# One-tile chunks, two hidden blocks in a PSUM bank and epsilon as a column of the masked sum, in top-k attention followed by an MLP

## The chip, the cores and the metric

The kernel runs on one core of one Trainium2 chip. The metric is the device time in microseconds; the time before is the median of three runs. The profile is one execution of the program taken by the hardware profiler. TensorE (PE) multiplies matrices, its weight loads are listed apart (PEld); VectorE (DVE), ScalarE (ACT) and GpSimd (POOL) work elementwise, and SyncE (SP) issues the transfers.

## The reference

Top-32 attention over 8 batches of 8 heads, 576 queries and keys, head dimension 64; the result, as 4608 tokens of 512, goes through an MLP of 2048 hidden units with a piecewise activation. Everything is float32.

```python
# q, k, v: (8, 8, 576, 64); w_in: (512, 2048); w_out: (2048, 512)
scores = scale * np.matmul(q, k.transpose(0, 1, 3, 2))
kth = np.partition(scores, -32, axis=-1)[..., -32:-31]
scores = np.where(scores >= kth, scores, -1e9)
attn = np.exp(scores - np.max(scores, axis=-1, keepdims=True))
attn = attn / (np.sum(attn, axis=-1, keepdims=True) + 1e-09)
x = np.matmul(attn, v)                    # then (B,H,S,D) -> (B*S, H*D)
h = x @ w_in
g = np.where(h >= 1, h, np.where(h <= -1, 0.0, (h + 1) ** 2 / 4))
out = g @ w_out
```

## The kernel before

A **step** treats one tile of 128 queries and two heads (a tail tile gathers the last 64 queries of two batches). There are 144 steps. In a step TensorE makes the scores, ScalarE scales them and takes the exponentials, VectorE finds the 32nd largest of each row, masks and sums, GpSimd divides by the sum, a transfer through DRAM transposes the weights, and TensorE multiplies by the values. Four steps (two for a tail tile) fill one tile `xT` of 128 tokens, and the MLP of that tile is then queued as small pieces of work, which are issued between the steps that follow. The weights of the MLP and some inputs arrive as 64-bit words and are converted during the first steps. The order on each engine is fixed when the program is built.

The top-k on VectorE works on half-width tiles: `more` is the larger, later the smaller, of two halves of the scores.

```python
nc.vector.tensor_tensor(out=more, in0=s[:, :, 0:SH], in1=s[:, :, SH:S], op=ALU.max)     # L294
nc.vector.max(out=eight(tops, i, 0), in_=more[:, i, :])                                  # L305, x2
for r in range(8, TOP_K, 8):                                                             # three rounds
    nc.vector.match_replace(...)                                                         # L321, x2
    nc.vector.max(out=eight(tops, i, r), in_=src[:, i, :])                               # L330, x2
nc.vector.tensor_tensor(out=less, in0=s[:, :, 0:SH], in1=s[:, :, SH:S], op=ALU.min)      # L332
nc.vector.max(...)                                                                       # L335, x2
nc.vector.tensor_tensor_scan(out=kth, ...)                                               # L337
for i in range(2):                                                                       # masked sum
    nc.vector.scalar_tensor_tensor(out=e[:, i, :], in0=s[:, i, :], scalar=last[i], in1=e[:, i, :],
                                   op0=ALU.is_ge, op1=ALU.mult, accum_out=z[:, i:i + 1]) # L344
nc.vector.tensor_scalar(z, z, 1e-9, None, ALU.add)                                       # L349
nc.vector.reciprocal(rz, z)                                                              # L350
# ... GpSimd: e *= rz (L357); ScalarE: two copies of e as 16-bit halves (L386); transfers (L388, L389)
```

The scores go through PSUM tiles of two banks, twice a step; the values and the MLP's first products share a pair of banks.

```python
sp = ps.tile([P, 2, BANK], F32, name="sp", tag="a", bufs=2)     # scores; transposes use the same tag
po = ps.tile([P, P], F32, name="po", tag="ph", bufs=2)          # values (L403, L411)
```

The MLP of a chunk, which is one tile or two:

```python
def hidden(f, c0, c1):                                          # block f of 128 hidden units
    ph = ps.tile([P, CW], F32, name="ph", tag="ph", bufs=2)[:, 0:c1 - c0]
    for kk in range(NK):                                        # L433
        nc.tensor.matmul(ph, w_in[:, kk, f * P:(f + 1) * P], xT[:, kk, c0:c1], ...)
    nc.scalar.activation(r, ph, AF.Relu, bias=half, scale=0.5)  # L437
    nc.scalar.activation(g, ph, AF.Relu, bias=minus, scale=1.0) # L445
    nc.gpsimd.tensor_scalar(r, r, 1.0, 0.0, ALU.min, ALU.max)   # L450
    nc.gpsimd.tensor_tensor(out=r, in0=r, in1=r, op=ALU.mult)   # L451
    nc.gpsimd.tensor_tensor(out=g, in0=r, in1=g, op=ALU.add)    # L452

def final(f):
    for i in range(len(tiles)):                                 # L458; py: a pair of banks
        nc.tensor.matmul(pys[i], gs[f][:, i * P:(i + 1) * P], w_out[:, f, :], ...)
        # after the last f: y = copy of py by ScalarE (L462), then the store

for x in range(NF + LAG):      # LAG = 4: final(x - 4) goes with hidden(x)
    ...
```

A matmul of float32 shows as two records in the trace, each with its weight load. In the values below, a unit is one product of 128 x 128 x 128: `hidden` of one tile has 4, `final` of one tile has 4, a tile has 128 and the program 4608.

Of the kernel before, what the change touches and what calls it, by code (L numbers as in the profile page):

```python
# [24 lines left out]
def kernel(  # L25
# [27 lines left out]
    NF = DFF // P  # L53
    CT = 2
    CW = CT * P
    LAG = 4
# [21 lines left out]
    for i in range(2):  # L78
        v_tails.append([const.tile([P, H, D], F32, name=f"v_tail{i}{x}") for x in range(2)])
        for x in v_tails[i]:  # L80
            nc.gpsimd.memset(x, 0.0)


# [83 lines left out]
    def run(ctx, paired):  # L167
        xtp = ctx.enter_context(tc.tile_pool(name="xtp", bufs=3))
        stage = ctx.enter_context(tc.tile_pool(name="stage", bufs=2))
# [97 lines left out]
        def scores(st):  # L267
            t, hp, kT, qT = st["t"], st["hp"], st["keys"]["kT"], st["qT"]
            st["s"] = s = att.tile([P, 2, S], F32, name="s", bufs=3)
            for hf in range(2):  # L270
                sp = ps.tile([P, 2, BANK], F32, name="sp", tag="a", bufs=2)
                c0, c1 = hf * SH, (hf + 1) * SH
                for i in range(2):
                    for j in ([i] if t < NT else [0, 1]):
                        d = slice(j * D, (j + 1) * D)
                        g = hp if t < NT else hp + i
                        o = sp[:, i] if t < NT else sp[j * TL:(j + 1) * TL, i]
                        for a0, a1, k0 in pieces(i, j, c0, c1):
                            nc.tensor.matmul(o[:, a0 - c0:a1 - c0], qT[d, g, :], kT[d, g, k0:k0 + a1 - a0],  # L279
                                             start=True, stop=True)  # L280
                nc.scalar.activation(s[:, :, c0:c1], sp[:, :, 0:SH], AF.Copy, scale=SCALE)  # L281
# [15 lines left out]
        def first_top(st):  # L297
            s = st["s"]
            if paired:
                pairs(st)  # L300
            st["tops"] = tops = att.tile([P, 2 * TOP_K], F32, name="tops", bufs=3)
            st["e"] = e = att.tile([P, 2, S], F32, name="e", bufs=3)
            nmax = att.tile([P, 2], F32, name="nmax")
            for i in range(2):
                nc.vector.max(out=eight(tops, i, 0), in_=(st["more"] if paired else s)[:, i, :])  # L305
            nc.scalar.activation(nmax, tops[:, 0:2 * SPLIT:SPLIT], AF.Copy, scale=-1.0)
            for i in range(2):
                nc.scalar.activation(e[:, i, :], s[:, i, :], AF.Exp, bias=nmax[:, i:i + 1])  # L308
                yield


        def weights(st, after):
            s, m, tops, e = st["s"], st["m"], st["tops"], st["e"]
            kth = att.tile([P, LAST + 1], F32, name="kth", bufs=3)
# [28 lines left out]
            for i in range(2):  # L343
                nc.vector.scalar_tensor_tensor(out=e[:, i, :], in0=s[:, i, :], scalar=last[i],  # L344
                                               in1=e[:, i, :], op0=ALU.is_ge, op1=ALU.mult,
                                               accum_out=z[:, i:i + 1])
            yield
            rz = att.tile([P, 2], F32, name="rz")
            nc.vector.tensor_scalar(z, z, 1e-9, None, ALU.add)  # L349
            nc.vector.reciprocal(rz, z)  # L350
            if st["by_tensor"]:
                st["rz"] = diag = (late or words).tile([P, 2, P], F32, name="diag", bufs=1)
                for i in range(2):
                    nc.scalar.activation(diag[:, i, :], ident, AF.Copy, scale=rz[:, i:i + 1])
            else:
                for i in range(2):
                    nc.gpsimd.tensor_scalar(e[:, i, :], e[:, i, :], rz[:, i:i + 1], 1.0, ALU.mult, ALU.mult)  # L357
            if paired:
# [36 lines left out]
        def values(st):  # L395
            t, hp, v_in, v_tl = st["t"], st["hp"], st["keys"]["v"], st["keys"]["v_tl"]
            wT = st["wT"]
            po = ps.tile([P, P], F32, name="po", tag="ph", bufs=2)
            if t < NT:
# [26 lines left out]

        def mlp(xT, tiles, pool, last):
            gs, pys = {}, {}

            def hidden(f, c0, c1):  # L430
                ph = ps.tile([P, CW], F32, name="ph", tag="ph", bufs=2)[:, 0:c1 - c0]
                for kk in range(NK):
                    nc.tensor.matmul(ph, w_in[:, kk, f * P:(f + 1) * P], xT[:, kk, c0:c1],  # L433
                                     start=(kk == 0), stop=(kk == NK - 1))

                r = pool.tile([P, CW], F32, name="r", bufs=2)[:, 0:c1 - c0]
                nc.scalar.activation(r, ph, AF.Relu, bias=half, scale=0.5)  # L437
                gs[f] = pool.tile([P, CW], F32, name="g", bufs=2 * LAG)
                g = gs[f][:, c0:c1]
                if last:  # L440
# [4 lines left out]
                nc.scalar.activation(g, ph, AF.Relu, bias=minus, scale=1.0)  # L445
                if converted < n_pieces and f % 2:
                    nc.scalar.activation(r, r, AF.Square)
                    nc.gpsimd.tensor_scalar(r, r, 1.0, 0.0, ALU.min, ALU.max)
                else:
                    nc.gpsimd.tensor_scalar(r, r, 1.0, 0.0, ALU.min, ALU.max)  # L450
                    nc.gpsimd.tensor_tensor(out=r, in0=r, in1=r, op=ALU.mult)  # L451
                nc.gpsimd.tensor_tensor(out=g, in0=r, in1=g, op=ALU.add)  # L452

            def final(f):
                for i in range(len(tiles)):
                    if f == 0:
                        pys[i] = ps.tile([P, DM], F32, name="py", tag="py", bufs=2)
                    nc.tensor.matmul(pys[i], gs[f][:, i * P:(i + 1) * P], w_out[:, f, :],  # L458
                                     start=(f == 0), stop=(f == NF - 1))
                    if f == NF - 1:  # L460
                        y = (late or words).tile([P, DM], F32, name="y", bufs=2)
                        nc.scalar.copy(y, pys[i])  # L462
                        for p0, p1, rows in rows_of(*tiles[i]):
                            nc.sync.dma_start(out=rows, in_=y[p0:p1])


            n_tiles, work = len(tiles), []
            for x in range(NF + LAG):
                if x < NF:
                    work.append((NK * n_tiles, needed(x, False), partial(hidden, x, 0, n_tiles * P)))  # L470
                if x >= LAG:
                    work.append((n_tiles * DM // P, needed(x - LAG, True), partial(final, x - LAG)))
            return work


        rounds, chunks = [], []
        for b in range(0, B, 2):
            a, c, tl = [(b, t) for t in range(NT)], [(b + 1, t) for t in range(NT)], (b, NT)
            rounds += a + [tl, (b + 1, NT)] + c
            if 0 < b and b + 2 < B:  # L480
                chunks += [a[0:2], a[2:4], [tl]] + ([c[0:2], c[2:4]] if b + 4 < B else [[x] for x in c])
            else:
                chunks += [[x] for x in a + [tl] + c]
        steps = []
        for b, t in rounds:
            tile_of = (b, t) if t < NT else (b - b % 2, t)
            ch = next(n for n, tiles in enumerate(chunks) if tile_of in tiles)
            col = chunks[ch].index(tile_of) * P + (TL if t == NT and b % 2 else 0)
            for hp in (range(NHP) if t < NT else range(0, NHP, 2)):
                steps.append((b, t, hp, ch, col))  # L490
# [7 lines left out]
        pending = deque()  # L498
        total, spent = sum(len(tiles) for tiles in chunks) * (NK * NF + NF * DM // P), 0
        converted, inspected, due = 0, 0, 0.0  # L500
# [28 lines left out]
        def advance(amount, until):  # L529
# [4 lines left out]
            while pending:  # L534
                cost, pieces, work = pending[0]
                if pieces > converted or usable[pieces] > pe_time + 0.5:
# [44 lines left out]
        def begin(m):  # L581
            b, t, hp, ch, col = steps[m]
            if ch not in xTs:
                xTs[ch] = xtp.tile([P, NK, CW], F32, name="xT")
            state.append(dict(m=m, t=t, hp=hp, keys=keys[b], qT=qTs[b, t], xT=(xTs[ch], col)))
# [27 lines left out]
        def values_until(m):  # L613
            nonlocal valued, pe_time
            while valued < min(m, n):
# [3 lines left out]
                if valued in ready:  # L619
                    ch = ready[valued]  # L620
                    pending.extend(mlp(xTs[ch], chunks[ch], mlp_pool, ch == len(chunks) - 1))
                valued += 1

        first_late = None
        for m in range(n + 2):
# [8 lines left out]
            for r in sorted(ready):  # L634
                if r + 3 > m and r >= valued:
                    share = min(share, left / (r + 3 - m))
                    left += len(chunks[ready[r]]) * (NK * NF + NF * DM // P)
            top_k, parts = None, [0] * SLOTS
# [8 lines left out]
            for slot in range(SLOTS):  # L647
# [24 lines left out]
                if slot == 4:  # L672
                    begin_at(m + 2)
                if slot == 5 and not early:
                    values_until(m - 1)
                if slot == (6 if early else 1):
# [63 lines left out]
```

## Time and profile before

| | before |
|---|---|
| median of three runs | 1665.99 us (1664.15 to 1668.44) |
| span of the profiled execution | 1666.6 us |
| mean granted TensorE clock | 0.972 |
| PE / PEld busy | 1540.7 / 1057.8 us |
| DVE busy | 1532.8 us |
| ACT busy | 1208.2 us |
| POOL busy | 1041.8 us |
| mean transfer rate | 137 GB/s |

A group line of the profile has the kernel's line, engine and operation, output and inputs, shape and count; after the bar the busy time and the mean length of one in ns; after the second bar the engine's idle time ahead of it and what ended it. Where instructions of an engine overlap, the busy time counts the overlap once. A line of the list of waits has the waiting engine and line, what ended the wait, the total in us, the number of waits and the longest. Line numbers are those of the kernel before unless another is named.

### The profile page before, as it was taken

Reading aid. Unit: us, or ns where it says so; the run is one execution under the profiler, and the core shown is the slowest. Engines: PE = TensorE matmul, PEld = TensorE weight load, DVE = VectorE, ACT = ScalarE, POOL = GpSimd, SP = SyncE. Lnnn points to the kernel's source line nnn. Section 1 sums busy time; section 2 is a strip of 40 time slices with the busy share of each in tenths; the row PEclk is TensorE's granted clock in tenths of the full one; section 3 lists DMA queues with packets and bytes.
Section 4 is the critical chain, followed back from the end, with each engine's and each line's share of the span. In section 5 each row is a group of like instructions: output and inputs, shape, how many; then the busy total and the mean of one; then the engine's idle time right before and its main releaser. Section 6 shows DMA issues by size and latency. Waiting matters only on the chain.

```text
span 1666.6 us, 32108 instructions
## 1 busy us (share of the span) xinstructions
PE 1540.7 (92%) x10157; PEld 1057.8 (63%) x10157; DVE 1532.8 (92%) x4587; ACT 1208.2 (72%) x2680; POOL 1041.8 (63%) x1918
## 2 busy tenths in 40 slices
PE   6586999999999999999999999999999999999998
PEld 4464666666666666666566666666666666666665
DVE  6999999999999999999999999999989998999942
ACT  5686677777777876787677777777777776777743
POOL 4675676666667645565454545577766676777750
PEclk6798999999999999999999999999999999999999
DMA  8333256555455556555555556545554544445420
GB/s 249 114 99 98 80 143 171 146 151 148 141 150 144 158 138 173 161 149 143 134 160 163 141 140 178 155 135 135 127 156 124 146 124 124 132 124 129 109 64 16
DMA packets 439061, 227.91 MB, mean 137 GB/s; under 512 B 393056, under 2 KB 401248, under 8 KB 438880
## 3 DMA queue, kind: packets, MB, share of 16 engines
q1 hardware_dynamic: 438880, 225.75, 49.7%
q8 instruction: 82, 1.34, 0.3%
q14 instruction: 99, 0.81, 0.2%
HBM read 62.91 MB, written 86.11 MB: 89 GB/s over the span
## 4 chain that ended last, share of the span: by engine, by line
PE 38%; DVE 37%; ACT 14%; POOL 5%; issue 4%; DMA 1%; SPq 0%; POOLq 0%; DVEq 0%; ACTq 0%
PE ph L433 15%; PE py L458 14%; DVE more L321 9%; DVE tops L330 8%; DVE e L344 6%; ACT halves L386 4%; PE sp L279 4%; PE po L403 4%; DVE seconds L335 3%; DVE more L332 3%; DVE tops L305 3%; ACT e L308 3%; DVE more L294 3%; POOL e L357 2%; ACT s L281 2%
## 5 line engine op out<-in xcount | busy, mean ns | idle before, releaser
L433 PEld LDWEIGHTS ph<-xT,w_in 128*128 128x128 f32 x3840 | 531.0, 193 | 222.7 <-issue 99.6
L433 PE MATMUL ph<-xT,w_in 128*128 128x128 f32 (+1 forms) x3840 | 604.6, 304 | 47.2 <-ACT g L445 43.4
L458 PE MATMUL py<-w_out,g 128*128 128x512 f32 x1152 | 573.4, 604 | 1.7 <-POOL w_out L146 0.9
L450 POOL TENSOR_SCALAR r<-r 128x128 f32<-128x128 f32 (+1 forms) x456 | 187.0, 410 | 408.7 <-ACT r L437 407.6
L437 ACT ACTIVATE r<-ph,half 128x128 f32<-128x128 f32 (+1 forms) x480 | 186.9, 389 | 273.9 <-PE ph L433 228.0
L321 DVE MATCH_REPLACE8 more<-tops,more 128x288 f32<-128x288 f32 x864 | 375.7, 442 | 0.0
L330 DVE MAX8 tops<-more 128x8 f32<-128x288 f32 x864 | 349.1, 445 | 0.0
L452 POOL TENSOR_TENSOR g<-r,g 128x128 f32<-128x128 f32 (+1 forms) x464 | 277.6, 598 | 36.4
L386 ACT COPY halves<-e 128x1152 uint16<-128x1152 uint16 x260 | 287.1, 1155 | 15.5 <-POOL e L357 14.7
L458 PEld LDWEIGHTS py<-w_out,g 128*128 128x128 f32 x1152 | 192.4, 191 | 117.6 <-issue 87.9
L451 POOL TENSOR_TENSOR r<-r 128x128 f32<-128x128 f32 (+1 forms) x456 | 239.2, 525 | 38.0
L344 DVE SCALAR_TENSOR_TENSOR e<-s,kth,e 128x576 f32<-128x576 f32 x288 | 249.9, 904 | 6.0
L357 POOL TENSOR_SCALAR e<-e,rz 128x576 f32<-128x576 f32 x260 | 215.1, 838 | 49.5 <-DVE rz L350 49.5
L308 ACT ACTIVATE e<-s,nmax 128x576 f32<-128x576 f32 x288 | 218.5, 770 | 4.7
L445 ACT ACTIVATE g<-ph,minus 128x128 f32<-128x128 f32 (+1 forms) x464 | 179.6, 387 | 0.0
L281 ACT ACTIVATE s<-sp 128x576 f32<-128x576 f32 x288 | 169.6, 640 | 5.4 <-PE sp L279 5.4
L279 PE MATMUL sp<-kT,qT 64*128 64x288 f32 x1024 | 163.1, 436 | 9.4 <-ACT kT L239 8.5
L403 PE MATMUL po<-wT,v_in 128*64 128x128 f32 x2048 | 143.9, 280 | 16.5 <-ACT g L445 11.3
L403 PEld LDWEIGHTS po<-wT,v_in 128*64 128x64 f32 x2048 | 111.4, 137 | 70.6 <-issue 21.7
L279 PEld LDWEIGHTS sp<-kT,qT 64*128 64x128 f32 x1024 | 90.2, 189 | 84.3 <-issue 52.3
L294 DVE TENSOR_TENSOR more<-s 128x576 f32<-128x576 f32 x144 | 112.4, 780 | 23.9 <-ACT s L281 23.5
L335 DVE MAX8 seconds<-more 128x8 f32<-128x288 f32 x288 | 118.3, 452 | 14.0
(89 smaller groups left out, 1331.0 us busy)
## 6 DMA issues: line engine op xcount, KB each, us to landing
rows<-halves SPq DMA_DIRECT2D x130, 576.0 KB, 2.8
raw<-in_moe_w_out_dram SPq DMA_DIRECT2D x52, 256.0 KB, 3.0
raw<-in_moe_w_in_dram SPq DMA_DIRECT2D x48, 256.0 KB, 3.0
k_in<-in_k_dram SPq DMA_DIRECT2D x64, 128.0 KB, 3.1
q_in<-in_q_dram SPq DMA_DIRECT2D x32, 256.0 KB, 3.3
v_in<-in_v_dram SPq DMA_DIRECT2D x8, 1024.0 KB, 6.4
out_dram<-y SPq DMA_DIRECT2D x32, 256.0 KB, 3.0
kT<-in_moe_w_in_dram SPq DMA_DIRECT2D x16, 256.0 KB, 4.2
```

The source lines that it names most:

```text
L279: nc.tensor.matmul(o[:, a0 - c0:a1 - c0], qT[d, g, :], kT[d, g, k0:k0 + a1 - a0], start=True, stop=True)
L308: nc.scalar.activation(e[:, i, :], s[:, i, :], AF.Exp, bias=nmax[:, i:i + 1])
L321: nc.vector.match_replace(out=rest[:, i, :], in_to_replace=eight(tops, i, r - 8), in_values=src[:, i, :], imm_value=LOWEST)
L330: nc.vector.max(out=eight(tops, i, r), in_=src[:, i, :])
L344: nc.vector.scalar_tensor_tensor(out=e[:, i, :], in0=s[:, i, :], scalar=last[i], in1=e[:, i, :], op0=ALU.is_ge, op1=ALU.mult, accum_out=z[ ...
L357: nc.gpsimd.tensor_scalar(e[:, i, :], e[:, i, :], rz[:, i:i + 1], 1.0, ALU.mult, ALU.mult)
L386: nc.scalar.copy(halves[:, :, i * S:(i + 1) * S], st["e"][:, i, :].bitcast(U16).rearrange("p (k t) -> p t k", t=2))
L403: nc.tensor.matmul(po[j * D:(j + 1) * D], v_in[:, h, c, :] if c < NT else v_tl[0][:, h, :], wT[:, block(j, c)], start=(c == 0), stop=(c == ...
L433: nc.tensor.matmul(ph, w_in[:, kk, f * P:(f + 1) * P], xT[:, kk, c0:c1], start=(kk == 0), stop=(kk == NK - 1))
L451: nc.gpsimd.tensor_tensor(out=r, in0=r, in1=r, op=ALU.mult)
L452: nc.gpsimd.tensor_tensor(out=g, in0=r, in1=g, op=ALU.add)
L458: nc.tensor.matmul(pys[i], gs[f][:, i * P:(i + 1) * P], w_out[:, f, :], start=(f == 0), stop=(f == NF - 1))
```

## The change

It has five parts.

1. **Chunks of one tile.** Before, the tiles of the middle batches went two at a time through the MLP, so that ScalarE and GpSimd worked on 256 columns, and the others alone with 128. Now all go alone.
2. **Two blocks in a bank.** `hidden` makes two blocks of 128 hidden units side by side in one PSUM bank, and ScalarE and GpSimd treat both in one instruction of 256 columns. The last tile keeps single blocks. The lag of four now counts groups of two.
3. **One unbroken stream, three banks.** The last second products of a tile are laid between the first groups of the next. Values and first products share three banks instead of two; second products have one instead of two.
4. **Values next to scores.** In the later part a step's values are issued directly behind scores, a slot earlier than before.
5. **Epsilon as a column.** The score and weight tiles get a column 576, with the largest number and 1e-9, set once; the masked sum runs over 577 columns, and the separate addition goes.

The diff, cut to its core:

```diff
-    CT = 2
-    CW = CT * P
+    GROUP = 2
...
+    scores_of, weights_of = [[const.tile([P, 2, S + 8], F32, name=f"{x}{i}") for i in range(3)] for x in ("s", "e")]
+    for i in range(3):
+        nc.gpsimd.memset(scores_of[i][:, :, S:S + 1], LARGEST)
+        nc.gpsimd.memset(weights_of[i][:, :, S:S + 1], 1e-9)
...
-                nc.vector.scalar_tensor_tensor(out=e[:, i, :], in0=s[:, i, :], scalar=last[i],
-                                               in1=e[:, i, :], op0=ALU.is_ge, op1=ALU.mult,
+                nc.vector.scalar_tensor_tensor(out=st["all"][1][:, i, :], in0=st["all"][0][:, i, :], scalar=last[i],
+                                               in1=st["all"][1][:, i, :], op0=ALU.is_ge, op1=ALU.mult,
                                                accum_out=z[:, i:i + 1])
             yield
             rz = att.tile([P, 2], F32, name="rz")
-            nc.vector.tensor_scalar(z, z, 1e-9, None, ALU.add)
             nc.vector.reciprocal(rz, z)
...
-            po = ps.tile([P, P], F32, name="po", tag="ph", bufs=2)
+            po = ps.tile([P, P], F32, name="po", tag="ph", bufs=3)
...
-            def hidden(f, c0, c1):
-                ph = ps.tile([P, CW], F32, name="ph", tag="ph", bufs=2)[:, 0:c1 - c0]
-                for kk in range(NK):
-                    nc.tensor.matmul(ph, w_in[:, kk, f * P:(f + 1) * P], xT[:, kk, c0:c1],
-                                     start=(kk == 0), stop=(kk == NK - 1))
+            def hidden(x):
+                ph = ps.tile([P, group, P], F32, name="ph", tag="ph", bufs=3)
+                for i in range(group):
+                    f = x * group + i
+                    for kk in range(NK):
+                        nc.tensor.matmul(ph[:, i], w_in[:, kk, f * P:(f + 1) * P], xT[:, kk],
+                                         start=(kk == 0), stop=(kk == NK - 1))
...
-                        pys[i] = ps.tile([P, DM], F32, name="py", tag="py", bufs=2)
+                    py.append(ps.tile([P, DM], F32, name="py", tag="py", bufs=1))
...
+            behind = []
+            while pending and pending[-1][3]:
+                behind.insert(0, pending.pop())
+            for x in range(NF // group + LAG):
+                if x < NF // group:
+                    pending.append((NK * group, needed(x * group + group - 1, False), partial(hidden, x), False))
+                if x < LAG:
+                    for _ in range(min(GROUP, len(behind))):
+                        pending.append(behind.pop(0)[0:3] + (False,))
+                else:
+                    for f in range((x - LAG) * group, (x - LAG + 1) * group):
+                        pending.append((DM // P, needed(f, True), partial(final, f), x >= NF // group))
...
-            if 0 < b and b + 2 < B:
-                chunks += [a[0:2], a[2:4], [tl]] + ([c[0:2], c[2:4]] if b + 4 < B else [[x] for x in c])
-            else:
-                chunks += [[x] for x in a + [tl] + c]
+            chunks += a + [tl] + c
...
                 if slot == 4:
                     begin_at(m + 2)
-                if slot == 5 and not early:
-                    values_until(m - 1)
+                    if not early:
+                        values_until(m - 1)
```

## The prediction

> **What bounds the kernel now.** I read the busy table first, then the busy time by stage, then the waits of the late stage, then VectorE's instructions one by one.
>
> ```profile
> PE 1540.7 (92%) x10157; PEld 1057.8 (63%) x10157; DVE 1532.8 (92%) x4587; ACT 1208.2 (72%) x2680; POOL 1041.8 (63%) x1918
> ```
>
> TensorE and VectorE stand at the same 92%, so the page alone does not say which one sets the pace. The view by stage does better (its columns: stretch, then busy us of PE, PEld, DVE, ACT, POOL, then clock and DMA):
>
> ```profile
> 0.00:200.00 200.00, 142.27 (x919) 106.95 (x920) 183.00 (x528) 135.74 (x332) 123.39 (x203) 0.83 0.43 126
> 200.00:550.00 350.00, 329.39 (x2338) 226.47 (x2338) 337.00 (x1011) 271.23 (x613) 239.70 (x469) 0.99 0.56 151
> 550.00:1100.00 550.00, 534.13 (x3204) 353.01 (x3200) 533.70 (x1625) 407.63 (x814) 309.46 (x506) 0.99 0.57 152
> 1100.00:1603.00 503.00, 478.55 (x3368) 331.53 (x3364) 468.07 (x1386) 372.16 (x861) 357.24 (x711) 1.00 0.48 130
> 1603.00:1667.00 64.00, 56.37 (x345) 39.80 (x341) 10.99 (x40) 21.45 (x64) 12.05 (x32) 0.97 0.03 11
> ```
>
> From 200 to 1100 us VectorE is busy 96 to 97% of the time; from 1100 to 1603 only 93%; after 1603 it is done and TensorE alone works for 63 us. VectorE does the same work in each of the 144 steps (one step is one pair of heads of one tile of queries), so I measured the step as the distance between two reciprocals (one per step, first at 32.1, last at 1603.5 us):
> steps 0 to 14: 12.79 us; 14 to 45: 10.69; 45 to 95: 10.50; 95 to 143: 11.16; over 14 to 143: 10.79. Nineteen steps lie below 10.25, the shortest full ones at 10.19 to 10.20: that is VectorE's step when nothing disturbs it.
>
> What lies above 10.20 has two sources. One is wait: in 1100 to 1600 us the list of waits has
>
> ```profile
> DVE more L294 <- ACT s L281: 20.6, 16, 3.9
> PEld ph L433 <- ACT g L445: 32.7, 39, 2.6
> PE ph L433 <- ACT g L445: 17.6, 24, 1.8
> ```
>
> so VectorE waits 20.6 us for scores that TensorE and ScalarE bring late, 0.46 us a step; in 550 to 1100 it waits for nothing, in 200 to 550 for 2.9 us. TensorE in its turn waits for ScalarE to empty a bank of first products (ph). The other source is stretch: the same VectorE instruction is sometimes longer. The masked sum (L344) has a shortest time of 0.806 us and a median of 0.819 before 1100 and 0.940 after. Mean minus shortest, summed over L294, L332, the two L344, L337 and the addition of epsilon (L349), gives 0.40 us a step in 200 to 550, 0.35 in 550 to 1100, 0.58 in 1100 to 1600. The parts add up: 10.20 + 0.40 + 0.09 = 10.69; 10.20 + 0.35 = 10.55 (measured 10.50); 10.20 + 0.58 + 0.46 = 11.24 (11.16). So VectorE bounds, and the rest is what others do to it.
>
> **What the Trainium skill says.** "SBUF — State Buffer", Who interferes with whom: a VectorE instruction with two SBUF inputs contends with a GpSimd instruction that reads SBUF, and the later one blocks until the first is done. The stretched lines L294, L332 and L344 have two SBUF inputs and the maxima (L330, 437 to 455 ns) with one never stretch: the trace agrees. "VectorE: DVE Perf Modes", Rules for kernel authors: for chained operations, minimise their count, not their waits; removing a 128x2 addition is that. "Perfetto Trace Analysis", Identifying the Most-Contended Engine: matmul busy time says little about how near TensorE is to its limit; indeed I count below 9.7 us of dense TensorE work in a step whose busy time is 10.2. "PSUM — Partial Sum Buffer", Specifications (TRN2): eight banks of 2 KiB. Score tiles take four, so 2 + 2 for ph and py become 3 + 1.
>
> **The change part by part.**
>
> Epsilon. Column 576 of the score tile holds the largest number, of the weight tile 1e-9, so the masked sum over 577 columns adds epsilon itself. L349 goes, 144 times. In the trace:
>
> ```profile
> 563.94 0.08 DVE L344 DVE_READ_ACCUMULATOR e<-s,kth,e 128x1 f32 x1
> 564.06 0.17 DVE L349 TENSOR_SCALAR z<-z 128x2 f32<-128x2 f32 x1
> 564.26 0.17 DVE L350 RECIPROCAL rz<-z 128x2 f32<-128x2 f32 x1
> 564.35 0.07 DVE L321 MATCH_VALUE_LOAD more<-tops,more 128x8 f32 x1
> ```
>
> From L349's start to the reciprocal's is 0.20 to 0.21 us undisturbed, 0.25 on average over steps 14 to 143 (L349 itself is stretched at times), 0.19 in the first 14. One column more in L344 is 1/576 of 0.82 us, twice a step: 0.003 us. The undisturbed step becomes 10.20 - 0.21 = 9.99 us.
>
> Two blocks of 128 hidden units in one bank. The groups of instructions, shapes kept apart:
>
> ```profile
> L433 PE MATMUL ph<-xT,w_in 128*128 128x128 f32 x3072 | 415.2, 281 | 36.9 <-ACT g L445 35.8 <-ACT xT L416 1.0
> L433 PE MATMUL ph<-xT,w_in 128*128 128x256 f32 x768 | 189.5, 394 | 10.3 <-ACT g L445 7.6 <-ACT xT L416 2.7
> L445 ACT ACTIVATE g<-ph,minus 128x128 f32<-128x128 f32 x368 | 134.3, 365 | 0.0
> L445 ACT ACTIVATE g<-ph,minus 128x256 f32<-128x256 f32 x96 | 45.3, 472 | 0.0
> L451 POOL TENSOR_TENSOR r<-r 128x128 f32<-128x128 f32 x360 | 168.2, 467 | 30.0
> L451 POOL TENSOR_TENSOR r<-r 128x256 f32<-128x256 f32 x96 | 71.0, 740 | 8.0
> ```
>
> Before, 24 of 36 tiles ran alone with 128-column work and 12 ran as pairs with 256. After, every tile but the last has 256-column work on ScalarE and GpSimd. ScalarE for first products: 141.1 + 134.3 + 45.8 + 45.3 = 366.5 us before; 280 x (0.477 + 0.472) = 266 and about 11 for the last tile after: 90 us less. GpSimd: 200.4 + 168.2 + 143.0 + 77.2 + 71.0 + 44.0 = 704 us before; 280 x (0.458 + 0.740 + 0.804) = 560 after: 144 us less. Neither engine is the bound, so these count only through what they do to the others. TensorE's count rises, as a 256-column matmul becomes two of 128: but eight records of 256 columns take 1.73 to 1.83 us from start to start (900 to 908 us), and eight of 128 columns take 0.87 in the last stage: the same per column. No cost there.
>
> Stretch and waits then: everywhere the 256-column form of the stage 550 to 1100, with its 0.35 us of stretch, less the 0.05 that belonged to L349: 0.30. The waits for scores should nearly go: three ph banks give ScalarE one group more of delay, and the work is spread more evenly. Counted in the instruction order of both programs in units of one 128x128x128 product (0.217 us each), the steps after 1100 us have 34.1 units before and about 32.5 after, since the earlier steps no longer run at 28 to 32. I leave 0.06 for waits. Step: 9.99 + 0.30 + 0.06 = 10.35 us.
>
> TensorE must fit in that. Dense, from the trace: 32.5 units x 0.217 = 7.05, scores 1.15, values 1.25, transposes of queries and keys about 0.25: 9.7 us. It fits, with 0.65 to spare.
>
> Values directly behind the scores, and the end of one tile's stream laid between the next tile's first products: fewer edges at which TensorE has only one kind of work. I count this within the small rest of waits.
>
> The end: after the last values 208 units are left before and 200 after, so 8 x 0.217 = 1.7 us less. The last tile's own 128 units have to come after the last weights either way.
>
> **Sum.** First 14 steps: 14 x 0.19 = 2.7 us less. Steps 14 to 143: 129 x (10.79 - 10.35) = 56.8 us less. End: 1.7 less. Together 61 us: 1666 - 61 = 1605 us.
>
> **Rivals.** (1) *TensorE becomes the bound.* In 550 to 1100 it is busy 10.21 us of a 10.52-us step, and if that were true work, not modelled ends and hidden waits, a step could not fall below some 10.3 plus the waits, about 10.5: 129 x 0.29 = 37 less, 1625 us. Against it: the dense count of 9.7.
> (2) *The single py bank.* The next tile's sums can start only once ScalarE has copied the last ones out (y, 0.587 us); only one group of first products (8 units, 1.74 us) lies between. ScalarE often sits in a pair of 1.155-us copies (L386), so TensorE may stall by about a microsecond for each of 36 tiles: if none of it is hidden, 36 us, 1640. In its favour: ScalarE is busy 74%; against it, TensorE's slack of 0.65 us a step, four steps a tile.
> (3) *Longer GpSimd instructions stretch VectorE more.* 0.74 and 0.80 us instead of 0.47 and 0.55 block longer each time; L344 alone is stretched by 0.19 us a step in 550 to 1100 and by 0.10 in 200 to 550. The sums over all lines (0.35 against 0.40) speak against it. It would cost 0.1 us a step, 13 us.
> (4) *Better than the sum:* no waits, less stretch, a step of 10.15: 1580 us.
>
> **Range and chances.** The centre is 1605. Rival 1 or 3 in part gives 1618 to 1628, rival 4 gives 1580; I take 1582 to 1630. Two per cent is 1633 us; only the py bank in full reaches past it, and I see nothing that adds more than the removed addition takes away.
>
> **What would show it.** Right: no 128x2 addition on VectorE, a mean step of 10.3 to 10.4 in every stage after 200 us and no longer 11.2 late; waits of L294 for scores under 8 us in all; GpSimd busy about 900 us, ScalarE about 1120; an end of about 61 us after the last reciprocal. Wrong: py matmuls idle behind the y copy (rival 2), VectorE waiting for scores in all stages with TensorE at 99% (rival 1), L344 with a higher mean than its 904 ns (rival 3).

## The result, and the profile after

The changed kernel takes 1611.12 us (median of four runs, 1608.12 to 1613.25) against 1666.18 before: a ratio of 0.9668, with a 95% interval of 0.9648 to 0.9688, or 55 us less. The lines of the changed kernel that matter are L300 for L294 (first use of `more`), L350 for L344 (masked sum), L355 for L350 (reciprocal), L441 and L464 for L433 and L458 (first and second products), L445, L452, L457 to L459 for the elementwise work of the MLP.

The busy table of the changed kernel, in the page's first part:

```profile
PE 1522.4 (94%) x10925; PEld 1086.5 (67%) x10925; DVE 1503.8 (93%) x4443; ACT 1142.2 (71%) x2308; POOL 871.4 (54%) x1376
```

ScalarE lost 66 us and GpSimd 170; VectorE lost 29, and its share rose. By stage (stretch, then PE, PEld, DVE, ACT, POOL busy, clock, DMA):

```profile
0.00:200.00 200.00, 143.11 (x922) 108.87 (x923) 182.03 (x512) 132.46 (x308) 114.61 (x183) 0.80 0.43 125
200.00:550.00 350.00, 345.12 (x2515) 244.77 (x2514) 338.24 (x1001) 259.76 (x512) 194.91 (x309) 1.00 0.58 155
550.00:1100.00 550.00, 545.16 (x4040) 387.47 (x4040) 534.92 (x1604) 413.61 (x815) 308.62 (x487) 0.99 0.58 156
1100.00:1550.00 450.00, 435.10 (x3147) 308.01 (x3145) 438.03 (x1292) 318.68 (x628) 246.13 (x386) 0.99 0.51 138
1550.00:1612.00 62.00, 53.87 (x312) 37.39 (x309) 10.59 (x37) 17.69 (x49) 7.10 (x13) 0.97 0.03 11
```

VectorE is now busy 97% in the late stage too, where it had 93%. TensorE stands at 97 to 99%. The waits of VectorE for scores over the whole run, before and now, are

```profile
DVE more L294 <- ACT s L281: 23.5, 20, 3.9
DVE more L300 <- ACT s L287: 2.5, 2, 2.2
```

And where epsilon was added, VectorE's instructions in order of time (start, length) now read

```profile
1500.77 0.08 DVE L350 DVE_READ_ACCUMULATOR e<-s,kth,e 128x1 f32 x1
1500.88 0.17 DVE L355 RECIPROCAL rz<-z 128x2 f32<-128x2 f32 x1
1500.96 0.07 DVE L327 MATCH_VALUE_LOAD more<-tops,more 128x8 f32 x1
```

0.11 us from the start of the accumulator's read to that of the reciprocal, where it was 0.32.

From the reciprocals of each step the time of the run is taken apart: the first 14 steps, 129 steps of a mean length, and what follows the last reciprocal. The step again is VectorE's undisturbed 10.20 us (9.99 without the addition), plus stretch (mean minus shortest length of its instructions with two inputs, its scan and its small additions), plus the time it sat idle for others. The sum is compared with the measured step. The same was done for every kernel that follows. Steps and tails are those of the profiled execution. That execution lies within 3 us of the median everywhere but in the run without GpSimd's MLP work, whose profiled execution took 1592.5 us.

| kernel | median us | ratio to before, 95% | step measured | undisturbed + stretch + waits | after the last reciprocal |
|---|---|---|---|---|---|
| before | 1666 | 1 | 10.79 | 10.20 + 0.43 + 0.17 | 63.1 |
| **changed** | 1611.1 | 0.9668 (0.9648 to 0.9688) | 10.38 | 9.99 + 0.40 + 0.02 | 61.4 |
| before, with epsilon column | 1656.4 | 0.9941 (0.9921 to 0.9961) | 10.72 | 9.99 + 0.45 + 0.29 | 63.9 |
| the same, chunks of one tile | 1719.3 | 1.0322 (1.0291 to 1.0352) | 11.21 | 9.99 + 0.52 + 0.67 | 62.1 |
| changed, no epsilon column | 1635.8 | 0.9814 (0.9795 to 0.9834) | 10.57 | 10.20 + 0.40 + 0.00 | 58.6 |
| changed, 2 + 2 banks | 1611.8 | 0.9674 (0.9646 to 0.9701) | 10.39 | 9.99 + 0.42 + 0.01 | 61.4 |
| changed, values a slot later | 1605.2 | 0.9635 (0.9610 to 0.9659) | 10.36 | 9.99 + 0.38 + 0.02 | 59.1 |
| changed, no stream | 1603.9 | 0.9629 (0.9612 to 0.9645) | 10.37 | 9.99 + 0.40 + 0.01 | 56.9 |
| changed, one block | **1597.4** | 0.9584 (0.9564 to 0.9603) | 10.32 | 9.99 + 0.33 + 0.02 | 58.0 |
| one block, 2 + 2 banks | 1614.6 | 0.9688 (0.9670 to 0.9706) | 10.46 | 9.99 + 0.45 + 0.03 | 59.3 |
| one block, no stream | 1640.3 | 0.9857 (0.9835 to 0.9879) | 10.64 | 9.99 + 0.42 + 0.24 | 56.1 |
| one block, values a slot later | 1612.8 | 0.9682 (0.9668 to 0.9696) | 10.40 | 9.99 + 0.39 + 0.04 | 59.7 |
| changed, GpSimd's MLP work left out | 1586.0 | 0.9515 (0.9495 to 0.9535) | 10.28 | 9.99 + 0.03 + 0.27 | 62.3 |
| changed, two replacements left out | 1592.6 | 0.9559 (0.9530 to 0.9588) | 10.26 | 9.15 + 0.72 + 0.39 | 67.4 |

The sum meets the measured step within 0.03 us in all fourteen kernels. The sum only tells where VectorE's time went; what a part of the change is worth is seen by undoing it.

### The profile page after: what moved, and what is told of

The parts are those of the page before. It is cut to its first block, busy times and chain, and to the rows that moved or that the text cites. A ratio compares the mean times of both kernels' runs of the same rounds, so it can differ in the third digit from the quotient of the medians.

```text
span 1611.4 us, 32433 instructions
## 1 busy us (share of the span) xinstructions
PE 1522.4 (94%) x10925; PEld 1086.5 (67%) x10925; DVE 1503.8 (93%) x4443; ACT 1142.2 (71%) x2308; POOL 871.4 (54%) x1376
## 4 chain that ended last, share of the span: by engine, by line
DVE 49%; PE 42%; ACT 3%; issue 2%; DMA 2%; POOL 1%; SPq 0%; DVEq 0%; POOLq 0%; ACTq 0%
PE ph L441 16%; PE py L464 14%; DVE more L327 12%; DVE tops L336 10%; DVE e L350 8%; PE sp L285 5%; PE po L408 4%; DVE seconds L341 4%; DVE more L338 4%; DVE tops L311 4%; DVE more L300 4%; DMA wT<-rows 2%; DVE kth L343 1%; DVE bits L147 1%; ACT halves L391 1%
## 5 line engine op out<-in xcount | busy, mean ns | idle before, releaser
L441 PEld LDWEIGHTS ph<-xT,w_in 128*128 128x128 f32 x4608 | 556.5, 193 | 112.5 <-issue 78.9
L441 PE MATMUL ph<-xT,w_in 128*128 128x128 f32 x4608 | 579.1, 279 | 11.0 <-ACT xT L421 10.2
L464 PE MATMUL py<-w_out,g 128*128 128x512 f32 x1152 | 559.9, 603 | 4.0 <-ACT y L467 3.0
L457 POOL TENSOR_SCALAR r<-r 128x256 f32<-128x256 f32 x276 | 123.0, 446 | 522.2 <-ACT r L445 521.5
L445 ACT ACTIVATE r<-ph,half 128x256 f32<-128x256 f32 (+1 forms) x296 | 138.9, 469 | 254.8 <-PE ph L441 227.1
L464 PEld LDWEIGHTS py<-w_out,g 128*128 128x128 f32 x1152 | 194.5, 192 | 134.5 <-issue 127.3
L350 DVE SCALAR_TENSOR_TENSOR e<-s,kth,e 128x577 f32<-128x577 f32 x288 | 251.9, 912 | 6.0
L459 POOL TENSOR_TENSOR g<-r,g 128x256 f32<-128x256 f32 x280 | 228.1, 815 | 22.0
L458 POOL TENSOR_TENSOR r<-r 128x256 f32<-128x256 f32 x276 | 186.2, 675 | 23.0
L452 ACT ACTIVATE g<-ph,minus 128x256 f32<-128x256 f32 x280 | 131.7, 471 | 0.0
L338 DVE TENSOR_TENSOR more<-s 128x576 f32<-128x576 f32 x144 | 122.9, 853 | 4.9
```

The lines of the kernel that those rows point to most:

```text
L350: nc.vector.scalar_tensor_tensor(out=st["all"][1][:, i, :], in0=st["all"][0][:, i, :], scalar=last[i], in1=st["all"][1][:, i, :], op0=ALU. ...
L441: nc.tensor.matmul(ph[:, i], w_in[:, kk, f * P:(f + 1) * P], xT[:, kk], start=(kk == 0), stop=(kk == NK - 1))
L464: nc.tensor.matmul(py[0], gs[f // group][:, f % group], w_out[:, f, :], start=(f == 0), stop=(f == NF - 1))
```

## The experiments

### The epsilon column, done alone and undone alone

**Alone in the kernel before:**

```diff
-            st["s"] = s = att.tile([P, 2, S], F32, name="s", bufs=3)
+            (tiles s and e with a column 576, set once, as in the change)
-                nc.vector.scalar_tensor_tensor(out=e[:, i, :], in0=s[:, i, :], ..., in1=e[:, i, :], ...)
+                nc.vector.scalar_tensor_tensor(out=st["all"][1][:, i, :], in0=st["all"][0][:, i, :], ...)
-            nc.vector.tensor_scalar(z, z, 1e-9, None, ALU.add)
```

> The kernel before with the epsilon column alone: 577-column masked sum, no 128x2 addition, everything else as before. Theory A (VectorE's chain sets the pace; each step is 9.99 us undisturbed instead of 10.20): where VectorE doesn't wait (steps 14 to 95) 0.23 us a step, 19 us; late (steps 95 to 143) VectorE waits 0.46 us a step for scores, so that some of the saving turns into wait: 4 to 10 us. Together 23 to 29 us less, about 1640. Theory B (TensorE is as much the bound, and the gain of the whole change comes from the MLP's new form): under 10 us less, with the waits of L300 (more) for scores grown by as much as L349 took.

1656.4 us, about 10 less: Theory B's number. VectorE's waits for scores in that run:

```profile
DVE more L300 <- ACT s L287: 38.6, 32, 4.1
```

Fifteen us more than before. The late steps did not move at all (11.19 us, 11.16 before), the middle ones by 0.17. Of the 0.21 us that VectorE saved in a step, 0.12 became waiting for scores, 0.02 stretch and 0.07 time. Theory A's picture of the kernel before, with VectorE the bound and TensorE at ease, is too simple.

**Undone in the changed kernel:**

```diff
-  out=st["all"][1][:, i, :], in0=st["all"][0][:, i, :], ..., in1=st["all"][1][:, i, :]
+  out=st["e"][:, i, :], in0=s[:, i, :], ..., in1=st["e"][:, i, :]
+            nc.vector.tensor_scalar(z, z, 1e-9, None, ALU.add)
             nc.vector.reciprocal(rz, z)
```

> The changed kernel with the epsilon column undone: the masked sum over 576 columns and the 128x2 addition back. Theory A: VectorE waits nowhere in the changed kernel, so the addition costs its full 0.21 to 0.25 us in each of 129 steps: 27 to 32 us more, about 1640. Theory B: under 10 us more, since the MLP's form made the gain. If both this run and the run with epsilon alone give some 27, the other parts are worth about 27 too, and the parts simply add.

1635.8 us, 24.6 more than the changed kernel, a little under the 27 to 32 of Theory A. The step grew by 0.19 us and VectorE waited nowhere. So the same column is worth 10 us in one kernel and 25 in the other, and the parts do not add: column alone 10, the rest alone 30 (1666 to 1636), both 55. The 15 us over come from the waits that the rest of the change removes: only without them does a shorter VectorE step shorten the program.

### One tile a chunk, without the rest

```diff
 # the kernel before with the epsilon column
-            if 0 < b and b + 2 < B:
+            if False:
                 chunks += [a[0:2], a[2:4], [tl]] + (...)
```

> The kernel before with the epsilon column and with all chunks of one tile, one block in a bank, two banks for first products, two for second, no unbroken stream, values a slot later. Counted in the instruction order, the steps after 1100 us then have 32.4 units instead of 34.4, as in the changed kernel. If the epsilon column alone brought only 10 us because TensorE had too much to do in the late steps, the evener load lets the late steps fall from 11.2 to about 10.7 us: 20 to 25 us less than with the column alone, 1632 to 1637. Rival (the two banks and the edges between tiles make TensorE wait, not the load): less than 8 us, 1650 or more, with TensorE waiting for ScalarE's L450 as before.

A miss in both directions: 63 us *more* than with the column alone. The load is as even as in the changed kernel (32.2 units in the late steps of both, 33.9 with the column alone). But the late steps came down by no more than 0.07 us (11.19 to 11.12), and the middle ones rose to them (10.33 to 11.29). So the load by itself was not what made the late steps slow; my reading of the 34 units there was wrong. The late steps of the kernel before are those in which the tiles went alone already. What happens is seen in TensorE's instructions at one tile's start (start, length, records, idle time ahead):

```profile
801.49 3.88 PE L438 MATMUL ph<-xT,w_in 128*128 128x128 f32 x32
805.30 1.24 PE L285 MATMUL sp<-kT,qT 64*128 64x288 f32 x8
806.84 1.16 PE L438 MATMUL ph<-xT,w_in 128*128 128x128 f32 x8 [0.29 <-ACT g L450]
809.41 1.09 PE L408 MATMUL po<-wT,v_in 128*64 128x128 f32 x16 [1.42 <-ACT g L450]
```

Four blocks of first products come one behind the other (32 records), then the scores; then the next block and the values, which use the same two banks, wait for ScalarE to read the blocks out. (From 804.05 to 806.26 ScalarE makes the two copies of `e`.) The list of TensorE's waits from 200 to 1530 us has

```profile
PE ph L438 <- ACT g L450: 57.2, 68, 2.7
PE po L408 <- ACT g L450: 21.5, 18, 3.5
```

against 38.7 and 9.8 with paired tiles. A late TensorE brings late scores, and VectorE waited for them in the same stretch:

```profile
DVE more L300 <- ACT s L287: 86.6, 67, 4.3
```

In the kernel before, pairs had half as many such starts; where its tiles went alone, early and late, it waited. That is the wait that the change had to remove.

### Which part removes it

From the single-tile run (1719) to the changed kernel (1611) four parts act: two blocks in a bank, the stream, the third bank, the place of the values. I undid each in the changed kernel.

```diff
-    GROUP = 2                                   # one block in a bank
+    GROUP = 1
```

`GROUP = 1` changes two things besides the width: the lag goes back from eight blocks to four, and TensorE gets first products in pieces of four units and not eight. No run parts these from the width.

> The changed kernel with one hidden block in a bank (GROUP = 1): ScalarE and GpSimd work on 128 columns for every tile, three banks, stream and epsilon column as changed. Units per step stay (32.5 on average). ScalarE gets some 90+45 us more work and GpSimd some 140+70 us more. Theory A: VectorE is stretched by up to 0.1 us a step more and waits for scores a little as ScalarE empties banks later: 15 to 45 us more than the changed kernel, with GpSimd busy about 1080 us. Rival (three banks and the stream, not the wide instructions, removed the waits): within 8 us of the changed kernel.

Faster than the changed kernel by 14 us, against both expectations in sign: the best run of all. GpSimd is busy 1109.6 us and ScalarE 1237.9, some 240 and 95 more than in the changed kernel, and yet VectorE is stretched less, 0.33 us a step against 0.40. The groups of the changed kernel first,

```profile
L350 DVE SCALAR_TENSOR_TENSOR e<-s,kth,e 128x577 f32<-128x577 f32 x288 | 251.9, 912 | 6.0
L459 POOL TENSOR_TENSOR g<-r,g 128x256 f32<-128x256 f32 x280 | 228.1, 815 | 22.0
L458 POOL TENSOR_TENSOR r<-r 128x256 f32<-128x256 f32 x276 | 186.2, 675 | 23.0
```

then those with one block:

```profile
L350 DVE SCALAR_TENSOR_TENSOR e<-s,kth,e 128x577 f32<-128x577 f32 x288 | 241.8, 877 | 6.0
L459 POOL TENSOR_TENSOR g<-r,g 128x128 f32<-128x128 f32 x560 | 306.2, 547 | 43.9
L458 POOL TENSOR_TENSOR r<-r 128x128 f32<-128x128 f32 x552 | 272.8, 494 | 46.1
```

The masked sum is 35 ns shorter on average (877 against 912), twice a step. How the lengthening comes about is seen in the changed kernel:

```profile
708.73 0.61 POOL L458 TENSOR_TENSOR r<-r 128x256 f32<-128x256 f32 x1
708.75 1.21 DVE L350 SCALAR_TENSOR_TENSOR e<-s,kth,e 128x577 f32<-128x577 f32 x1
709.42 1.12 POOL L459 TENSOR_TENSOR g<-r,g 128x256 f32<-128x256 f32 x1
```

GpSimd's square has started 0.02 us before the masked sum and keeps its usual 0.61 us; the masked sum, which comes second, takes 1.21 instead of 0.82. The sum of GpSimd that starts while the masked sum runs takes 1.12 instead of 0.73. So the later one is lengthened, as the prediction had it, and the 288 masked sums of the run agree: 214 start while no GpSimd instruction runs, and none of them is more than 0.015 us over the shortest (0.808), though in 13 a GpSimd instruction starts. The other 74 start into a running one and are longer by 0.38 us on average. With one block 151 start into a running one, but lose only 0.12 us each: 18 us in all instead of 28. The longer GpSimd instructions here meet VectorE's less often and cost more each time. How often they meet depends on the order: with other parts of the change undone it is 72 to 100 meetings of 0.30 to 0.35 us with two blocks, and 194 to 218 of 0.13 to 0.14 with one, where the stretch is 0.39 to 0.45. Of the 14 us, 129 x 0.06 = 8 lie in the steps, 2.5 in the first 14 and 3.4 behind the last reciprocal.

```diff
-            po = ps.tile(..., tag="ph", bufs=3)   # and ph; py bufs=1
+            po = ps.tile(..., tag="ph", bufs=2)   # and ph; py bufs=2
```

> The changed kernel with two banks for first products and values and two for second products, as before. If the third bank took TensorE's waits for ScalarE away, they come back: TensorE waits for L452 some 0.3 to 0.5 us a step, and 15 to 30 us more than the changed kernel. If the wide groups and the stream did it (a group in a bank gives ScalarE 1.74 us), under 6 us more; the single second-product bank's waits for the y copy, 3.0 us in all in the changed kernel, go.

No difference (1611.8). With two blocks in a bank the third bank is not needed: TensorE's matmuls wait 6.3 us for L452, no more.

```diff
-                        pending.append((DM // P, needed(f, True), partial(final, f), x >= NF // group))
+                        pending.append((DM // P, needed(f, True), partial(final, f), False))
```

> The changed kernel without the unbroken stream: a tile's last eight second products stand together, then the next tile's first four groups (8 blocks, 32 units) follow one another with no second products between. Theory (the edges between tiles were what single tiles suffered from): four groups take TensorE 7 us and ScalarE 3.8 us plus what stands between them, so with three banks and groups of two TensorE is held up by about a microsecond a tile: 15 to 40 us more than the changed kernel. Rival (three banks and wide groups suffice): under 6 us more.

7 us *less* than the changed kernel. The steps are the same (10.37), and VectorE hardly waits (0.01); the gain is in what follows the last reciprocal (56.9 us, 61.4 with the stream) and the first 14 steps (2.5 us). With two blocks in a bank the stream brings nothing.

```diff
                     begin_at(m + 2)
-                    if not early:
-                        values_until(m - 1)
+                if slot == 5 and not early:
+                    values_until(m - 1)
```

> The changed kernel with the values a slot later again, apart from the scores. The waits for the transposed weights (8 us in all in the changed kernel) go; switching once more between kinds of matmul and a later xT cost about as much. Within 5 us of the changed kernel either way; if the place of the values mattered for the banks (values take one of the three between first products), 8 us or more slower.

6 us less, just beyond the 5 of the expectation; the waits of TensorE for xT fall from 9.5 to 2.6 us and for transposed weights from 6.6 to 2.1.

So with two blocks in a bank each of the three other parts can go without a wait coming back, and each is worth nothing or costs a little. Whether two blocks would do with all three gone was not run. But with one block the run is faster still, so there something else removes the waits. I undid the same parts there (the same edits, on top of GROUP = 1).

> One block in a bank, stream and place of the values as changed, two banks for first and two for second products. From the single-tile run of the kernel before (1719 us) to one block in a bank with the changed rest (1597) are 122 us, made by three parts: stream, third bank, values next to scores. If the stream is the cure, this run comes within 12 us of 1597; if the third bank is, it stays above 1640, with waits of TensorE for L452 over 40 us.

> One block in a bank, three banks and place of the values as changed, no unbroken stream. The counterpart of the run before: if the stream is the cure, above 1640; if the third bank is, within 12 us of 1597. If both are needed, both runs lie well above.

> One block in a bank with the values a slot later than in the changed kernel: the two undone parts that were each faster than the changed kernel (14 and 6 us) put together. If they add: 1591. TensorE's floor, shown by the runs with less GpSimd or VectorE work, is 1586 to 1593, so not below 1586; if TensorE already is the floor of the run with one block, 1595 to 1598.

1614.6, 1640.3 and 1612.8 us. The stream is the cure here, though not alone: without it 43 us are lost, and the waits of VectorE for scores are back,

```profile
DVE more L300 <- ACT s L287: 31.8, 20, 3.2
```

while two blocks without the stream have 0.8 us of them in the same stretch, 200 to 1530 us. The third bank is worth 17 us: without it the step has 0.12 us more stretch but VectorE hardly waits more, which neither of my two readings expected (TensorE's matmuls wait 13.1 us for xT instead of 5.0). The values a slot later lose 15, where with two blocks they gained 6: the two undone parts did not add, and the hope of 1591 failed.

### How far TensorE's own floor is

Two runs take work from the others and leave TensorE's as it is.

```diff
 # GpSimd's MLP work left out: g is max(h - 1, 0) alone
                 nc.scalar.activation(g, ph, AF.Relu, bias=minus, scale=1.0)
-                if converted < n_pieces and x % 2: ...
-                    nc.gpsimd.tensor_scalar(r, r, 1.0, 0.0, ALU.min, ALU.max)
-                    nc.gpsimd.tensor_tensor(out=r, in0=r, in1=r, op=ALU.mult)
-                nc.gpsimd.tensor_tensor(out=g, in0=r, in1=g, op=ALU.add)
```

> The changed kernel with GpSimd's three instructions of each group of first products left out (clamp, square and sum; the second products take max(h-1,0) alone, so the output is not the reference's). It measures what GpSimd's work costs VectorE. Theory A: the 0.40 us of stretch a step comes from GpSimd; the MLP's share of it (537 of 871 us busy) goes and a step falls from 10.38 to 10.1 to 10.15 us: 30 to 37 us less, 1575 to 1580, with L350 near its 0.81 us. Rival (TensorE is the floor just below 10.3 us): under 12 us less, and VectorE begins to wait for scores. Rival 2 (the stretch has another origin): L350's mean stays at 0.91 us.

1586.0 us, 25 less. All stretch has gone, although GpSimd still divides the weights (it is busy 303.6 us):

```profile
L350 DVE SCALAR_TENSOR_TENSOR e<-s,kth,e 128x577 f32<-128x577 f32 x288 | 224.9, 819 | 6.0
```

So the stretch of 0.40 us a step came from the MLP's part of GpSimd's work, as Theory A had it. But only 0.10 us of it became time in a step (the first 14 steps gave 6 us more). More than half the steps are now at 10.00 us (their median), the rest are held up: VectorE waits for scores 34.6 us in all.

```diff
 # two replacements left out: the second eight are found twice
-                for i in range(2):
+                for i in range(0 if r == 16 else 2):
                     nc.vector.match_replace(...)
```

> The changed kernel with the second round's two replacements left out (L327 for r = 16: the second round of maxima then finds the same eight again, so the weights are not the reference's). VectorE's undisturbed step falls by 0.84 us to 9.15; nothing else changes. It asks where TensorE's own floor lies. By the dense count of the prediction (9.7 us) a step comes to 9.75 to 9.9 us: 60 to 80 us less than the changed kernel, 1530 to 1550. By the run without GpSimd's MLP work, in which VectorE began to wait, the floor is 10.1 to 10.25: 17 to 35 us less, 1576 to 1594, with VectorE waiting about 0.6 us a step for scores.

1592.6 us. VectorE had 0.84 us less to do in a step, and the step fell by 0.12. The rest went into 0.32 us more stretch and 0.37 more wait:

```profile
DVE more L300 <- ACT s L287: 51.8, 51, 5.3
```

Two different reliefs of VectorE end at 10.26 and 10.28 us a step, and in both TensorE begins the last step's values within 0.3 us of the same moment, though VectorE's last reciprocal is 4.5 us earlier in the second (first line: GpSimd's MLP work left out; second: two replacements left out):

```profile
1539.51 1.09 PE L408 MATMUL po<-wT,v_in 128*64 128x128 f32 x16
1539.82 1.09 PE L408 MATMUL po<-wT,v_in 128*64 128x128 f32 x16
```

In steps 14 to 143 TensorE's records cover 10.16 and 10.12 us a step, so it is almost never idle. Since their ends are modelled, this alone would not prove it; together these are strong signs that TensorE's floor, in this order of work, lies there: 0.1 us under the step of the changed kernel. The fastest kernel here that does the whole work has 10.32.

## Why the prediction was right, point by point

The time (1611 against 1605, range 1582 to 1630) holds, and so does the saved addition, which makes up most of it. Two terms were mis-sized, and the waits fell for another reason than the one given; that their number came true is in part luck.

- *The undisturbed step of 9.99 us*: right. The shortest full steps of the changed kernel are 9.99 to 10.00.
- *Waits fall from 0.17 to 0.06 us*: right, 0.02, but neither reason given for it stands. With two blocks in a bank two banks do as well as three (0.01), and an evener load by itself raised the waits (0.29 to 0.67). Either the two blocks or the stream keeps them away, given the third bank and the place of the values.
- *Stretch falls to 0.30 us*: wrong, 0.40. It was taken from the stage of paired tiles as if 256-column work on GpSimd stretched VectorE less. That held only in the stage it was taken from: 0.29 in steps 45 to 95, but 0.47 in 14 to 45 and 0.48 in 95 to 143. No order that was run with the whole work came to 0.30. The 0.10 us x 129 = 13 us are more than the whole difference from the centre.
- *Rival 3 (longer GpSimd instructions block longer)*: right in size, 0.1 us a step over the predicted 0.30, and the runs bear its mechanism out. Its sign came too, though barely: a mean of 912 ns for the masked sum, 904 before. A meeting cost 0.17 us on average before and 0.38 after, while the meetings fell from 155 to 74. The numbers held against it do not come out of the trace: in 200 to 550 us the stretch of the kernel before is 0.45 us a step and not 0.40, and the masked sum's part of it 0.15 and not 0.10 (0.17 and not 0.19 in 550 to 1100).
- *First 14 steps 2.7 us less*: 0.6 (12.79 to 12.75 us a step). The masked sum there grew from 869 to 956 ns on average in 32 to 208 us, which took back most of it.
- *The end 1.7 us less*: 1.7 (63.1 to 61.4).
- *Sum*: 129 x (10.79 - 10.38) = 53 us instead of 57, with 0.6 and 1.7.
- *TensorE has 0.65 us to spare*: wrong. Dense counting gave 9.7; the two relieved runs stop at 10.26 and 10.28. Rival 1 named the right floor (about 10.3) and was only not reached. The busy time, which the prediction set aside, had said so: 10.21 us of TensorE a step in the middle stage.
- *The single py bank (rival 2)*: nothing. TensorE waits 3.0 us for the y copy in 200 to 1550 us, and two banks give the same time.
- *The late stage*: predicted to come down to the others, and it did (11.16 to 10.42), but the reason given, an evener load, fell: with an even load alone the late steps are 11.12 us. What mattered was how ScalarE and TensorE meet at a tile's start.
- *The busy times of GpSimd (about 900) and ScalarE (about 1120)*: 871 and 1142.

The time behind the last reciprocal (56 to 62 us with single tiles, 67 in one run) differs only by how late TensorE makes the last values. From their last record to the end, with the same 200 units left, it is 50.2 to 50.9 us in every kernel with single tiles; that record comes 5.9 to 16.9 us after the last reciprocal.

What remains open: why moving the values one slot gains 6 us with two blocks and loses 15 with one. The stretch moves with it (0.40 to 0.38, 0.33 to 0.39). With one block the masked sums that start into a running GpSimd instruction rise from 151 to 194; no run set that place on purpose.

## What to carry to other kernels

Two engines that each stand above 90% can trade their slack: here shortening one showed in the time only as far as the other did not hold it up, so the same 0.21 us a step was worth 10 us in one kernel and 25 in the other. Find the floor of the second engine by taking work from the first, not by adding up its dense instructions. And a part of a change proves itself only by being undone: here the two blocks in a bank and the stream were each a cure for the same wait, and the version with one block is 14 us faster than the one with both.

## What the runs showed of the hardware that was not expected

In the changed kernel a masked sum on VectorE was lengthened only when a GpSimd instruction was already running at its start (74 of 288, by 0.38 us on average); the 13 into which one started kept their length, and there the GpSimd instruction was the longer one, by 0.34 us on average. In total 65% of the GpSimd work, 568 us, cost VectorE 0.37 us of stretch a step, 48 us. Giving GpSimd 256 columns at a time instead of 128 cut its busy time from 1109.6 to 871.4 us and halved these meetings (151 to 74), but each cost three times as much (0.12 to 0.38 us), so that VectorE was stretched by 0.07 us a step more. Over all orders that were run with the whole work and single tiles, the stretch was 0.33 to 0.52 us with one block in a bank and 0.38 to 0.42 with two.
